# Values on shared PSUM banks, an earlier start for scores and transposes, and no filler matmuls, in a windowed attention with two MLPs

## The chip, the cores and the metric

The kernel runs on one core of a Trainium2 chip. The metric is device time in microseconds (us), the median of a few runs; lower is better. The kernel before takes 647.86 us (median of three runs, 647.62 to 649.16). The profile is one more execution, of 647.93 us.

## The reference

The input is `q`, `k`, `v` of shape (2, 8, 768, 64): 2 batches, 8 heads, 768 tokens, 64 values a head, in float32. Attention keeps, for each token, the last 128 tokens (`window`) and the first 4 tokens (`n_sink`):

```python
scores = scale * np.matmul(q, k.transpose(0, 1, 3, 2))
keep = is_sink | in_window
scores = np.where(keep, scores, -1000000000.0)
a = np.exp(scores - np.max(scores, axis=-1, keepdims=True))
a = a / (np.sum(a, axis=-1, keepdims=True) + 1e-09)
x = np.matmul(a, v)          # then (1536, 512): all tokens by heads * 64
h = x @ w_in                 # 512 -> 2048
g = np.where(h >= 1, h, np.where(h <= -1, 0.0, (h + 1) ** 2 / 4))
x = g @ w_out                # 2048 -> 512
g2 = np.maximum(x @ w2_in, 0.0) ** 2
out = g2 @ w2_out
```

`q` and `k` are scaled so that scores are large and the softmax is sharp. The weights come as float64.

## The kernel before

**Units.** The attention is cut into 24 units `(b, j, c)`: batch `b`, 256 tokens `j` of 3, and a pair of heads `c` of 4. A unit goes through this chain, on all engines:

- `turn` (L646): TensorE transposes the unit's keys and queries into a PSUM tile `tp`; `turn_copy` (L662) copies them to `k` in SBUF on VectorE (for the first unit half of it on ScalarE).
- `scores` (L671): for each half `u` of the tokens and each head `e` one matmul of `k` into a PSUM bank.
- `least` (L685, VectorE) takes scores against a mask into `p`; `powers` (L697, ScalarE) takes exponentials; `norm` (L704, VectorE) and `weigh` (L709, GpSimd) divide by the sums.
- `turn_p` (L724): TensorE transposes the probabilities into a bank `tx`; `turn_p_copy` (L735, ScalarE) copies them to `pt`, a pool of 4 buffers. Units with `j > 0` also transpose the four sink columns (`turn_s`, L740).
- `values_of` (L753): the products of values and probabilities, into `av`; `rows_high` (L773, ScalarE) and `rows_low` (L776, VectorE) split the result into two parts, `x`, in the format that the MLPs multiply.

**The MLPs.** Each product is made of three matmuls of high and low parts. The hidden layer is L371, the output L445. Four blocks of 256 tokens and two of 512 of the first MLP are mixed into the attention; all later steps are of 512 tokens.

**The order.** Everything on the fast path is written out by a planner (`Planner.run`, L171): each task has an engine, a duration (`COST`), and a priority (`KEYS` by the step of the unit, `ADJUST` by the task's number); at each step it takes the task that can start first. So each engine has one fixed order, and an instruction that waits holds back all behind it on its engine. `SLOTS` says how many buffers of each kind there are; a task that takes one is placed when one is free.

**Before the branch.** The kernel first reads `window` and `n_sink` and computes a flag; all engines load it (L1296) and branch to the fast path (L1298) or to a dense one. Ahead of the branch stand the masks, `warm_pe` matmuls of the identity (`WARM`), and the first unit's `turn` and `turn_copy`.

**PSUM.** The core has 8 banks. On the fast path two (`psf`) serve the MLPs and the second scores of the first eight units, two (`sc`) the other scores, one (`tp`) the transposes of keys and queries, two (`tx`) the transposes of probabilities, and one (`av`) the values, whose two halves are taken in turn by `c % 2`. After the attention all eight go to the MLPs.

**Filler matmuls.** Where the planner expects TensorE to be idle ahead of the first MLP task, `warm_gaps` (L1080) puts matmuls of the identity (`warm_in`, L889) into the order, so many that they should fill the gap. They write the unused last 128 columns of the latest scores' bank.

Of the kernel before, what the change touches and what calls it, by code (L numbers as in the profile page):

```python
# [8 lines left out]
F32 = mybir.dt.float32  # L9
# [6 lines left out]
PSUM = bass.MemoryType.PSUM  # L16

P = 128
# [13 lines left out]
WARM = 2, 4, 0  # L32
# [7 lines left out]
PSF, SCB, TPB, TXB = 2, 2, 1, 2  # L40
SPARE = 8
HALF = 256
SLOTS = dict(
    q=2, v=VB, k=KB, p=PB, pt=PTB, sm=4, sp=2, st=2, vs=1, av=2, sc=SCB, tp=TPB, tx=TXB, f=PSF,
# [4 lines left out]
    q=-314.28, v=162.85, kd=-162.17, kp=-309.38, tp=385.01, tpc=274.06, kp0=136.26, s0=0.28,  # L49
    m0=-70.13, e0=432.00, s1=0.64, m1=-191.77, e1=84.03, n=246.73, pm0=968.58, sp0=52.16,  # L50
    pm1=-172.01, sp1=-270.90, x0=-19.43, xc0=-212.43, x1=131.81, xc1=314.82, ts=-83.58,
    tsc=-150.73, av=453.64, xh=50.99, xl=-384.16, vs=-330.44, vc=-0.51, k1=-379.64, k2=-168.85,
)
STEPS = [
    (0, 0, -62.81, 256), (0, 256, 307.34, 256), (0, 512, 147.48, 256), (0, 768, 419.78, 256),
    (1, 0, -294.09, 512), (1, 512, 423.75, 512),
]
SPREAD = 57.03, 346.62
LOADS = [132.01, -205.46, 680.35, 143.62, -478.23, -80.53]
PARTS = [-20.40, 0.98, 33.92, 370.05, -721.81, 284.53]  # L60
START = dict(SP=4080.0, PE=6900.0, ACT=6550.0, DVE=6650.0, POOL=6850.0)
LEAD = 390.62, 134.87
# [7 lines left out]
    yl=("POOL", 690, 740, 0), yl5=("POOL", 1240, 1290, 0),  # L70
    tp=("PE", 436, 620, 0), s=("PE", 640, 709, 0), ss=("PE", 415, 492, 0), x=("PE", 436, 620, 0),
# [186 lines left out]
class Weights:  # L258
# [59 lines left out]
    def part(self, key, h, tmp):  # L318
        for _, f in self.parts(key, h, tmp):
            f()  # L320

# [261 lines left out]
class Attention:  # L583


    def __init__(self, nc, loads, ident, pools):
        self.nc, self.loads, self.ident, self.po = nc, loads, ident, pools
        self.kt, self.st, self.vs, self.spare = {}, {}, {}, None

    def go_on(self, pools, ffn):  # L590
        nc, self.po, self.ffn = self.nc, pools, ffn
        self.av = pools["av"].tile([P, 512], F32, name="av")
        self.sink_p, self.sink_t = [], []
        for i in range(2):
            t = pools["one"].tile([P, 2, 3, 32], F32, name=f"sink_p{i}")
            nc.gpsimd.memset(t, 0.0)
            self.sink_p.append(t)
            self.sink_t.append(pools["one"].tile([96, 2 * P], F32R, name=f"sink_t{i}"))
# [47 lines left out]
    def turn(self, b, j, c):  # L646
        nc, po = self.nc, self.po
        banks = 2 if po["tag"] == "f" else 1
# [22 lines left out]
    def scores(self, b, j, c, u, banks=None):  # L671
# [5 lines left out]
        for e in range(2):  # L677
            nm = f"s_{st['nm']}_{u}_{e}"
            t = self.ffn.bank(nm, banks[e]) if banks else po["sc"].tile([P, 512], F32, tag="s", name=nm)
            self.spare, ps = t[:, 3 * P :], t[:, :wid]  # L680
# [104 lines left out]
    def plan(self, line):  # L785
# [3 lines left out]
        for n, unit in enumerate(UNITS):  # L789
# [30 lines left out]
            if n:  # L820
                h = hold("tp")
                t = add("tp", key("tp"), at(self.turn), [d["q"]], [h], [raw[g]] if g in raw else [])
# [10 lines left out]
            for i in range(2):  # L833
                small = "s" if j + i == 0 else ""
                banks = [hold("f"), hold("f")] if i == 1 and n < SPARE else None
                hs = banks or [hold("sc"), hold("sc")]
                first = add(
                    "s" + small, key(f"s{i}"), at(self.scores, i, banks),
# [12 lines left out]
            sp, stt, av = hold("sp"), hold("st"), hold("av")  # L851
# [228 lines left out]
def warm_gaps(order, nc, at):  # L1080
    out, last, begun = [], START["PE"], False
    for t in order:
        if t.engine == "PE":
            begun = begun or t.kind == "mm"
            count = int((t.start - last - 250) / 225)
            if count > 0 and not begun:
                out.append((lambda c=count: warm_in(nc, at, c), False))
            last = t.start + t.step
        out.append((t.emit, any(h.pool in LATE and h.slot >= SLOTS[h.pool] for h in t.takes)))
    return out  # L1090


def fast_path(tc, nc, io, half, at, psf, masks):
    with ExitStack() as ctx:
# [22 lines left out]
        apools = dict(tag="m", vs=right("avs", 1), pt=right("apt", PTB))  # L1117
        apools.update(one=right("aone", 1), k=right("ak", KB), p=right("ap", PB), sm=right("asm", 4))
        for nm, bufs in (("sc", SCB), ("tp", TPB), ("tx", TXB), ("av", 1)):
            apools[nm] = actx.enter_context(tc.tile_pool(name=nm, bufs=bufs, space=PSUM))  # L1120
        apools["tp"] = [apools["tp"]]
# [3 lines left out]
        def open_late():  # L1125
# [4 lines left out]
            pools["psum"] += one("psf1", LATE["f"], space=PSUM)  # L1130

        with tc.manual_schedule():
            opened = False
            order = fast_plan(at, ffn, weights, stage, wtmp)
            for emit, late in warm_gaps(order, nc, at):
# [3 lines left out]
                emit()  # L1139
# [127 lines left out]
def attention_ffn_kernel(ctx, tc, q, k, v, n_sink, window, w1i, w1o, w2i, w2o, out):  # L1267
# [4 lines left out]
    psf = [ctx.enter_context(tc.tile_pool(name=f"psf{i}", bufs=1, space=PSUM)) for i in range(PSF)]  # L1272
# [8 lines left out]
    at = Attention(nc, loads, ident, dict(k=one, tp=psf, tag="f"))  # L1281
    at.keys(*UNITS[0])
    with tc.manual_schedule(engines={mybir.EngineType.DVE, mybir.EngineType.PE}):
# [11 lines left out]
        warm_pe(nc, ident, psf, "d", WARM[2])  # L1295
# [38 lines left out]
```

## Time and profile before

| what | value |
|---|---|
| median of three runs | 647.86 us (647.62 to 649.16) |
| profiled execution | 647.93 us, span of its instructions 645.5 us |
| TensorE, busy by its records | 633.8 us (98%), 3266 matmul records |
| VectorE / ScalarE / GpSimd busy | 427.1 / 324.4 / 312.2 us |
| last matmul of the attention ends, long run of MLP matmuls begins | 172.61 us |
| the first MLP matmul begins | 37.74 us |

Between the span and the execution's own time lie 2.4 us, which no instruction fills. A float32 matmul counts as two records (two passes), a matmul in the MLPs' format as one. A record of a matmul is longer than the step from its start to the next one's, since matmuls overlap; so durations on TensorE are read here from start to start. Idle time stands in brackets behind a row, with the instruction that ended it.

### The profile page before, as it was taken

How to read it: one execution, taken by the hardware profiler on the slowest of the kernel's cores; microseconds unless marked ns; L12 is line 12 of the kernel's file. 1: busy time of each engine (PE TensorE's matmuls, PEld its weight loads, DVE VectorE, ACT ScalarE, POOL GpSimd, SP SyncE). 2: the span in 40 equal slices, each digit the busy share in tenths (PEclk: the TensorE clock that was granted, in tenths of full speed). 3: DMA queues.
4: the chain of work that ended last, by engine and by line, in shares of the span. 5: the costliest groups of instructions: out<-in, count | busy, mean ns of one | idle time of the engine just before them, and what ended most of it. 6: DMA issues, size and time to landing. Idle time of an engine off the chain costs nothing.

```text
span 645.5 us, 9230 instructions
## 1 busy us (share of the span) xinstructions
PE 633.8 (98%) x3266; PEld 513.7 (80%) x3266; DVE 427.1 (66%) x855; ACT 324.4 (50%) x695; POOL 312.2 (48%) x334
## 2 busy tenths in 40 slices
PE   8999999999999999999999999999999999999996
PEld 6676887777788888888888888888888888888885
DVE  6888999753578967487889877667676564222222
ACT  4799777952555443334445564554455345212320
POOL 5569557653364444153447985544455345212311
PEclk9999999999999999999999999999999999999999
DMA  5966533200022222023221123232222220001012
GB/s 135 251 172 159 131 75 112 67 18 2 11 81 73 69 94 65 1 65 98 66 85 53 60 66 96 67 98 81 84 68 95 65 86 13 1 1 49 17 65 73
DMA packets 63901, 47.91 MB, mean 74 GB/s; under 512 B 39652, under 2 KB 58340, under 8 KB 63844
## 3 DMA queue, kind: packets, MB, share of 16 engines
q1 hardware_dynamic: 62466, 46.56, 24.9%
q10 hardware_dynamic: 1378, 0.66, 0.3%
q8 instruction: 28, 0.46, 0.3%
q14 instruction: 29, 0.24, 0.1%
HBM read 43.01 MB, written 3.15 MB: 71 GB/s over the span
## 4 chain that ended last, share of the span: by engine, by line
PE 51%; DVE 1%; ACT 0%; issue 0%; POOL 0%
PE o L445 26%; PE h L371 25%; DVE u L384 0%; POOL g L402 0%; DVE u L409 0%; ACT u L378 0%; DVE wx L313 0%; ACT wx L293 0%; DVE wx L303 0%; ACT g L398 0%; DVE wx L310 0%; DVE acc L484 0%; DVE wx L311 0%
## 5 line engine op out<-in xcount | busy, mean ns | idle before, releaser
L371 PE MATMUL h<-x,w 128*128 128x512 f32 (+1 forms) x1224 | 272.8, 378 | 0.3 <-DVE u L409 0.3
L371 PEld LDWEIGHTS h<-x,w 128*128 128x128 f32 x1224 | 220.2, 188 | 44.9 <-issue 1.0
L402 POOL TENSOR_TENSOR g<-u,g 128x512 fp32r<-128x512 f32 (+1 forms) x102 | 137.5, 1351 | 161.7 <-ACT g L398 111.5
L315 POOL TENSOR_TENSOR w<-wx,w 128x512 fp32r<-128x512 f32 x64 | 84.0, 1312 | 129.3 <-ACT w L314 115.1
L445 PE MATMUL o<-g,w 128*128 128x512 f32 (+1 forms) x648 | 140.0, 368 | 0.1
L445 PE MATMUL o<-w,g 128*128 128x512 f32 (+1 forms) x588 | 132.7, 385 | 0.0
L445 PEld LDWEIGHTS o<-g,w 128*128 128x128 f32 x648 | 112.6, 188 | 22.4 <-POOL g L402 1.1
L445 PEld LDWEIGHTS o<-w,g 128*128 128x128 f32 x588 | 108.9, 188 | 22.1
L484 DVE TENSOR_TENSOR acc<-o,acc 128x512 f32<-128x512 f32 (+1 forms) x101 | 58.1, 596 | 59.8 <-PE o L445 59.7
L314 ACT CAST w<-wx 128x512 fp32r<-128x512 f32 x64 | 39.8, 621 | 90.5 <-DVE wx L313 90.4
L398 ACT CAST g<-u 128x512 fp32r<-128x512 f32 (+1 forms) x102 | 60.3, 595 | 38.8 <-DVE u L384 21.8
L384 DVE SCALAR_TENSOR_TENSOR u<-h,u 128x512 f32<-128x512 f32 x48 | 33.0, 688 | 52.4 <-ACT u L380 52.1
L310 DVE TENSOR_SCALAR wx<-wx 128x512 f32<-128x512 f32 x64 | 39.6, 619 | 41.9 <-ACT wx L293 41.3
L313 DVE CUSTOM_DVE_ANT_0 wx<-wx,wy 128x1024 uint16<-128x1024 uint16 x64 | 60.5, 945 | 4.3
L293 ACT ACTIVATE wx<-wraw 128x512 f32<-128x512 f32 x64 | 42.8, 669 | 34.5 <-POOL w L315 33.9
L384 DVE SCALAR_TENSOR_TENSOR u<-u 128x512 f32<-128x512 f32 (+1 forms) x54 | 42.9, 795 | 25.1 <-ACT u L378 24.8
L380 ACT ACTIVATE u<-h 128x512 f32<-128x512 f32 x48 | 28.6, 596 | 61.3 <-PE h L371 61.3
L714 POOL TENSOR_TENSOR p<-p,sm 128x520 f32<-128x520 f32 (+1 forms) x48 | 48.9, 1032 | 19.4 <-DVE sm L707 16.0
L378 ACT ACTIVATE u<-h,half 128x512 f32<-128x512 f32 (+1 forms) x54 | 34.5, 638 | 47.3 <-PE h L371 46.5
L303 DVE SCALAR_TENSOR_TENSOR wx<-wraw,wx 128x512 int32<-128x512 int32 x64 | 52.4, 819 | 1.3
L700 ACT ACTIVATE p<-p,sm 128x260 f32<-128x260 f32 (+1 forms) x96 | 46.9, 490 | 8.1 <-DVE sm L692 8.1
L297 ACT ACTIVATE wy<-wraw 128x512 int32<-128x512 uint32 x64 | 42.6, 665 | 0.0
(75 smaller groups left out, 487.6 us busy)
## 6 DMA issues: line engine op xcount, KB each, us to landing
wraw<-in_moe_w_in_dram SPq DMA_DIRECT2D x32, 512.0 KB, 3.7
wraw<-in_moe_w_out_dram SPq DMA_DIRECT2D x32, 512.0 KB, 3.7
vr<-in_v_dram SPq DMA_DIRECT2D x24, 128.0 KB, 2.5
qr<-in_q_dram SPq DMA_DIRECT2D x22, 128.0 KB, 3.4
kr<-in_k_dram SPq DMA_DIRECT2D x22, 128.0 KB, 2.9
out_dram<-acc SPq DMA_DIRECT2D x10, 256.0 KB, 2.0
k<-k SPq DMA_DIRECT2D x16, 64.0 KB, 1.9
qr<-in_q_dram SPq DMA_DIRECT2D x4, 64.0 KB, 2.9
```

The costliest lines, as they stand in the source:

```text
L293: nc.scalar.activation(s["x"], f32(s["r"][:, :, 1]), AF.Abs, scale=65536.0)
L303: nc.vector.scalar_tensor_tensor(s["xi"], s["r"][:, :, 1], -(1 << 31), s["xi"], ALU.bitwise_and, ALU.bitwise_or)
L313: ("c4", lambda: nc.vector.tensor_tensor(s["xi"], s["xi"], s["yi"], ALU.add)),
L315: ("cl", lambda: nc.gpsimd.tensor_tensor(s["w"][:, 1], s["x"], f32(s["w"][:, 0]), ALU.subtract)),
L371: nc.tensor.matmul(s["h"], w[:, a, c * P : (c + 1) * P], x[:, b, c, sl], start=n == 0, stop=n == 11)
L384: nc.vector.scalar_tensor_tensor(s["u"], a, 1.0 - ffn, s["u"], op, ALU.mult)
L398: nc.scalar.copy(halves()[0], s["u"])
L402: nc.gpsimd.tensor_tensor(g[1], s["u"], f32(g[0]), ALU.subtract)
L445: nc.tensor.matmul(s["o"], lhs, rhs, start=n + i + j == 0, stop=n == len(chunks) - 1 and i == 1)
L484: self.nc.vector.tensor_tensor(dst, o, dst, ALU.add)
L700: self.nc.scalar.activation(s, s, AF.Exp, bias=sm[:, 0, u, e : e + 1], scale=-1.0, accum_out=sm[:, 1, u, e : e + 1])
L714: self.nc.gpsimd.tensor_tensor(s, s, r, ALU.mult)
```

## The change

The values lose their own bank: `values_of` takes a tile of the `tx` pool, which grows from two banks to three (`TXB`), and gives it back when `rows_low` has read it. Three banks (two of `psf` and one, `turns`, for transposes of keys and queries) become fixed tiles that exist ahead of the branch, so that the first unit's first scores and the second unit's transposes can be issued there; in the plan they are empty tasks (`go`, `gp`). `WARM` puts two more identity matmuls ahead of those scores. The filler matmuls are gone. The planner's numbers (`KEYS`, `STEPS`, `LOADS`, `ADJUST` and others) are new, so the order of all engines is new; durations in `COST` and the sizes of the steps are the same.

```diff
-WARM = 2, 4, 0
+WARM = 2, 4, 2
-PSF, SCB, TPB, TXB = 2, 2, 1, 2
+PSF, SCB, TPB, TXB = 2, 2, 1, 3
-    q=2, v=VB, k=KB, p=PB, pt=PTB, sm=4, sp=2, st=2, vs=1, av=2, sc=SCB, tp=TPB, tx=TXB, f=PSF,
+    q=2, v=VB, k=KB, p=PB, pt=PTB, sm=4, sp=2, st=2, vs=1, sc=SCB, tp=TPB, tx=TXB, f=PSF,
-    q=-314.28, v=162.85, kd=-162.17, kp=-309.38, tp=385.01, tpc=274.06, kp0=136.26, s0=0.28,
+    q=-344.78, v=165.75, kd=-209.20, kp=-262.23, tp=336.12, tpc=272.18, kp0=138.55, s0=4.70,
...
+    go=("DVE", 0, 500, 0), gp=("PE", 0, 100, 0),
...
+class Bank:
+    def __init__(self, pool, name):
+        self.all = pool.tile([P, 512], F32, name=name)
+
+    def tile(self, shape, dtype, tag, name):
+        return self.all if len(shape) == 2 else self.all.rearrange("p (n w) -> p n w", w=shape[2])
...
-        self.av = pools["av"].tile([P, 512], F32, name="av")
...
-            t = self.ffn.bank(nm, banks[e]) if banks else po["sc"].tile([P, 512], F32, tag="s", name=nm)
-            self.spare, ps = t[:, 3 * P :], t[:, :wid]
+            if banks:
+                ps = self.ffn.bank(nm, banks[e])[:, :wid]
+            else:
+                ps = po["sc"][e].tile([P, 512], F32, tag=po["tag"], name=nm)[:, :wid]
...
-        av = st["av"] = self.av[:, c % 2 * 256 : c % 2 * 256 + 256]
+        av = self.po["tx"].tile([P, 512], F32, tag="m", name=f"av_{st['nm']}")[:, :256]
+        st["av"] = av
...
-            sp, stt, av = hold("sp"), hold("st"), hold("av")
+            sp, stt, av = hold("sp"), hold("st"), hold("tx")
...
-def warm_in(nc, at, count):
-    for i in range(count if at.spare is not None else 0):
-        nc.tensor.matmul(at.spare, at.ident, at.ident, start=True, stop=True)
...
-            for emit, late in warm_gaps(order, nc, at):
+            for t in order:
+                late = any(h.pool in LATE and h.slot >= SLOTS[h.pool] for h in t.takes)
...
-        warm_pe(nc, ident, psf, "d", WARM[2])
+        warm_pe(nc, ident, [tpb], "d", WARM[2])
+        at.scores(*UNITS[0], 0)
+        at.po.update(tp=[tpb])
+        at.turn(*UNITS[1])
     fast = nc.values_load(par.flag[0:1, 0:1], min_val=0, max_val=1)
```

Three places of the new order are shown as the built programs have them. In the names the batch's number is left out: `tp_0_1_0` is the transposes' tile of `j=0, c=1`, `s_0_1_0_0` the scores of `j=0, c=1`, half 0, head 0, `kr`, `qr` and `vr` are loaded keys, queries and values, `bank` and `turns` the fixed banks; `x2` is two equal rows.

TensorE around the branch, before:

```order
L655 MATMUL tp_0_0_1_128<-ident,qr_0_0_75 128x128 x2
L1296 TENSOR_LOAD par_flag
L1297 COMPARE_AND_BRANCH
L683 MATMUL s_0_0_0_0_280<-k_0_0_89 128x128
L683 MATMUL s_0_0_0_1_282<-k_0_0_89 128x128
L655 MATMUL tp_0_1_0_284<-ident,kr_0_1_84 128x128 x2
L655 MATMUL tp_0_1_0_284<-ident,qr_0_1_81 128x128 x2
L683 MATMUL s_0_0_1_0_299<-k_0_0_89 128x260
```

TensorE around the branch, of the change:

```order
L664 MATMUL bank_65<-ident,qr_0_0_74 128x128 x2
L903 MATMUL turns<-ident 128x128 x2
L694 MATMUL bank_64<-k_0_0_89 128x128
L694 MATMUL bank_65<-k_0_0_89 128x128
L664 MATMUL turns<-ident,kr_0_1_83 128x128 x2
L664 MATMUL turns<-ident,qr_0_1_80 128x128 x2
L1301 TENSOR_LOAD par_flag
L1302 COMPARE_AND_BRANCH
L694 MATMUL bank_64<-k_0_0_89 128x260
```

Two scores and four transposes have moved ahead of the load of the flag, behind two more identity matmuls.

TensorE at the first unit's values, before (the values `av` of the first unit come behind six filler matmuls):

```order
L683 MATMUL s_1_0_1_0_482<-k_1_0_327 128x260
L683 MATMUL s_1_0_1_1_484<-k_1_0_327 128x260
L731 MATMUL tx_0_3_0_490<-ident,p_0_3_0_370 128x128
L731 MATMUL tx_0_3_0_490<-ident,p_0_3_1_418 128x128 x2
L891 MATMUL s_1_0_1_1_484<-ident 128x128 x6
L768 MATMUL av<-pt_0_0_0_398,vr_0_0_439 64x256
```

TensorE at the first unit's values, of the change:

```order
L664 MATMUL turns<-ident,qr_1_0_268 128x128 x2
L742 MATMUL tx_0_1_0_402<-ident,p_0_1_0_303 128x128
L742 MATMUL tx_0_1_0_402<-ident,p_0_1_1_321 128x128 x2
L742 MATMUL tx_0_1_1_410<-ident,p_0_1_0_303 128x128
L742 MATMUL tx_0_1_1_410<-ident,p_0_1_1_321 128x128 x2
L780 MATMUL av_0_0_417<-pt_0_0_0_370,vr_0_0_328 64x256
```

The first values now follow the transposes of the second unit, before the fourth unit's transposes and before either score of `j=1, c=0`.

SyncE's loads behind the copies of the first two units' keys, before (`vr_0_0` are the first unit's values, `wraw` the first weights):

```order
L634 DMA k_1_1_340<-k_0_1_297 128x128
L573 DMA vr_0_2_345<-in_v_dram 128x4x64 x2
L634 DMA k_1_3_361<-k_0_3_348 128x128
L272 DMA wraw_0_0_372<-in_moe_w_in_dram 128x4x256
L573 DMA qr_1_2_387<-in_q_dram 128x4x64 x2
L573 DMA kr_1_2_390<-in_k_dram 128x4x64 x2
L634 DMA k_1_2_429<-k_0_2_381 128x128
L573 DMA vr_0_0_439<-in_v_dram 128x4x64 x2
```

The same place of the change:

```order
L643 DMA k_1_1_316<-k_0_1_284 128x128
L272 DMA wraw_0_0_323<-in_moe_w_in_dram 128x4x256
L583 DMA vr_0_0_328<-in_v_dram 128x4x64 x2
L643 DMA k_1_2_341<-k_0_2_331 128x128
L583 DMA vr_0_2_352<-in_v_dram 128x4x64 x2
L583 DMA qr_1_2_375<-in_q_dram 128x4x64 x2
L583 DMA kr_1_2_378<-in_k_dram 128x4x64 x2
```

The first unit's values have moved from the last of these loads to the third, and the first weights stand ahead of them.

## Rows read from the trace of the kernel before

**Rows 1.** Busy time by stretch: us (records) of each engine, clock, DMA share, GB/s.

```profile
0.00:10.85 10.85, 8.53 (x36) 6.69 (x36) 5.45 (x27) 3.16 (x9) 4.47 (x18) 1.00 0.65 147
10.85:37.74 26.89, 24.41 (x183) 16.73 (x181) 22.93 (x86) 20.99 (x71) 17.21 (x30) 1.00 0.82 207
37.74:172.61 134.87, 132.95 (x980) 103.30 (x978) 100.19 (x299) 95.84 (x276) 84.02 (x135) 1.00 0.31 81
172.61:310.64 138.03, 137.95 (x609) 113.76 (x607) 104.26 (x158) 63.47 (x104) 58.41 (x42) 1.00 0.21 65
```

**Rows 2.** The chain that ended last, its last two pieces: start, us, what.

```profile
629.58 11.04 PE o L445 x60
640.65 0.42 DVE acc L484
```

**Rows 3.** Timeline of TensorE around the branch: start, us, line, shapes, count.

```profile
6.91 0.80 PE L683 MATMUL s<-k 64*128 64x128 f32 x4 [0.61 <-DVE k L669]
7.64 0.69 PE L655 MATMUL tp<-ident,kr 128*128 128x128 f32 x2
...
8.68 1.67 PE L683 MATMUL s<-k 64*128 64x260 f32 x8
...
11.60 0.44 PE L655 MATMUL tp<-ident,kr 128*128 128x128 f32 x2
```

**Rows 4.** Timeline of GpSimd and VectorE around the branch.

```profile
5.45 0.29 POOL L923 COPY mask<-mask 128x128 f32<-128x128 f32 x1
6.10 0.45 POOL L596 MEMSET sink_p<- 128x192 f32 x2 [0.36 <-issue]
...
6.34 0.42 DVE L669 COPY k<-tp 128x256 f32<-128x256 f32 x1 [1.26 <-PE tp L655]
7.14 0.69 DVE L927 TENSOR_SCALAR mask<-mask 128x260 f32<-128x260 f32 x2 [0.37 <-POOL vsr L606]
...
9.96 0.43 DVE L692 CUSTOM_DVE_ANT_0 p<-s,mask 128x260 f32<-128x260 f32 x1 [0.47 <-PE s L683]
```

**Rows 5.** Timeline of TensorE at three stretches of filler matmuls (L891).

```profile
12.67 0.94 PE L891 MATMUL s<-ident 128*128 128x128 f32 x6 [0.41 <-DVE sm L692]
13.53 0.49 PE L683 MATMUL s<-k 64*128 64x128 f32 x4
...
20.97 0.55 PE L731 MATMUL tx<-ident,p 128*128 128x128 f32 x3
22.08 1.60 PE L891 MATMUL s<-ident 128*128 128x128 f32 x12 [0.56 <-DVE sm L692]
23.61 0.87 PE L768 MATMUL av<-pt,vr 128*64 128x256 f32 x8
...
27.06 0.87 PE L768 MATMUL av<-pt,vr 128*64 128x256 f32 x8
27.86 0.49 PE L891 MATMUL s<-ident 128*128 128x128 f32 x2
28.55 0.55 PE L731 MATMUL tx<-ident,p 128*128 128x128 f32 x3 [0.20 <-ACT pt L738]
28.94 0.38 PE L655 MATMUL tp<-ident,kr 128*128 128x128 f32 x2
```

**Rows 6.** Timeline of SyncE's queue: the issues of the first unit's values.

```profile
17.76 1.26 SPq L573 DMA_DIRECT2D vr<-in_v_dram  x2
```

**Rows 7.** The page's part on DMA issues: KB each, median us to landing.

```profile
vr<-in_v_dram SPq DMA_DIRECT2D x24, 128.0 KB, 2.5
```

**Rows 8.** Timeline of ScalarE and VectorE behind those stretches.

```profile
24.90 0.48 ACT L738 COPY pt<-tx 128x384 f32<-128x384 f32 x1 [1.37 <-PE av L768]
...
29.57 0.69 DVE L669 COPY k<-tp 128x512 f32<-128x512 f32 x1 [1.47 <-PE tp L655]
...
30.97 0.42 DVE L778 TENSOR_TENSOR x<-av,x 128x256 fp32r<-128x256 f32 x1
```

**Rows 9.** TensorE's waits from 37.74 to 172.61: us in total, times, longest.

```profile
PE ts L744 <- ACT pt L738: 0.3, 1, 0.3
```

More of the change, by code (lines that the diff above doesn't have):

```diff
@@ L48 @@
 KEYS = dict(
-    q=-314.28, v=162.85, kd=-162.17, kp=-309.38, tp=385.01, tpc=274.06, kp0=136.26, s0=0.28,
-    m0=-70.13, e0=432.00, s1=0.64, m1=-191.77, e1=84.03, n=246.73, pm0=968.58, sp0=52.16,
-    pm1=-172.01, sp1=-270.90, x0=-19.43, xc0=-212.43, x1=131.81, xc1=314.82, ts=-83.58,
-    tsc=-150.73, av=453.64, xh=50.99, xl=-384.16, vs=-330.44, vc=-0.51, k1=-379.64, k2=-168.85,
+    q=-344.78, v=165.75, kd=-209.20, kp=-262.23, tp=336.12, tpc=272.18, kp0=138.55, s0=4.70,
+    m0=-55.92, e0=490.71, s1=5.10, m1=-212.00, e1=112.49, n=200.32, pm0=935.74, sp0=37.11,
+    pm1=-189.91, sp1=-267.39, x0=-37.13, xc0=-221.23, x1=47.20, xc1=294.51, ts=3.54, tsc=-141.44,
+    av=437.63, xh=94.26, xl=-436.35, vs=-351.47, vc=28.84, k1=-354.91, k2=-81.86,
 )
 STEPS = [
-    (0, 0, -62.81, 256), (0, 256, 307.34, 256), (0, 512, 147.48, 256), (0, 768, 419.78, 256),
-    (1, 0, -294.09, 512), (1, 512, 423.75, 512),
-]
[L58 to L62, printed above, removed]
+    (0, 0, -52.86, 256), (0, 256, 267.55, 256), (0, 512, 185.85, 256), (0, 768, 401.71, 256),
+    (1, 0, -317.67, 512), (1, 512, 447.76, 512),
+]
+SPREAD = 52.75, 365.29
+LOADS = [114.00, -193.13, 635.31, 131.49, -461.22, -127.44]
+PARTS = [-17.08, 65.94, -2.94, 420.96, -785.29, 338.10]
+START = dict(SP=4080.0, PE=8100.0, ACT=6450.0, DVE=6950.0, POOL=6050.0)
+LEAD = 388.63, 141.49
 LAG = dict(PE=53, ACT=33, DVE=33, POOL=78, SP=40)
@@ L587, in __init__ @@
         self.nc, self.loads, self.ident, self.po = nc, loads, ident, pools
-        self.kt, self.st, self.vs, self.spare = {}, {}, {}, None
+        self.kt, self.st, self.vs = {}, {}, {}
     def go_on(self, pools, ffn):
         nc, self.po, self.ffn = self.nc, pools, ffn
-        self.av = pools["av"].tile([P, 512], F32, name="av")
         self.sink_p, self.sink_t = [], []
@@ L647, in turn @@
         nc, po = self.nc, self.po
-        banks = 2 if po["tag"] == "f" else 1
+        banks = len(po["tp"])
         ps = [
@@ L820, in plan @@
             if n:
-                h = hold("tp")
-                t = add("tp", key("tp"), at(self.turn), [d["q"]], [h], [raw[g]] if g in raw else [])
+                h, begun = hold("tp"), n == 1
+                t = add(
+                    "gp" if begun else "tp", key("tp"), (lambda: None) if begun else at(self.turn),
+                    [d["q"]], [h], [raw[g]] if g in raw else [],
+                )
                 d["tpc"] = add(
@@ L834, in plan @@
                 small = "s" if j + i == 0 else ""
-                banks = [hold("f"), hold("f")] if i == 1 and n < SPARE else None
+                begun = n + i == 0
+                banks = [hold("f"), hold("f")] if begun or i == 1 and n < SPARE else None
                 hs = banks or [hold("sc"), hold("sc")]
                 first = add(
-                    "s" + small, key(f"s{i}"), at(self.scores, i, banks),
+                    "go" if begun else "s" + small, key(f"s{i}"),
+                    (lambda: None) if begun else at(self.scores, i, banks),
                     [d["tpc"], d["kp"] if j + i else None, d.get("kd")], hs, [kt],
@@ L1077, in fast_plan @@
     return line.run()
[L1080 to L1090, printed above, removed]
 def fast_path(tc, nc, io, half, at, psf, masks):
@@ L1116, in fast_path @@
         at.loads.pool = right("araw", 2)
-        apools = dict(tag="m", vs=right("avs", 1), pt=right("apt", PTB))
+        apools = dict(tag="f", vs=right("avs", 1), pt=right("apt", PTB))
         apools.update(one=right("aone", 1), k=right("ak", KB), p=right("ap", PB), sm=right("asm", 4))
-        for nm, bufs in (("sc", SCB), ("tp", TPB), ("tx", TXB), ("av", 1)):
+        for nm, bufs in (("sc", SCB), ("tx", TXB)):
             apools[nm] = actx.enter_context(tc.tile_pool(name=nm, bufs=bufs, space=PSUM))
-        apools["tp"] = [apools["tp"]]
+        apools["sc"], apools["tp"] = [apools["sc"]] * 2, at.po["tp"]
         at.go_on(apools, ffn)
@@ L1129, in open_late @@
             pools["tmps"]["U"] = left("tmp1", LATE["U"], side="right")
-            pools["psum"] += one("psf1", LATE["f"], space=PSUM)
+            pools["psum"] += at.po["tp"] + one("psf1", LATE["f"] - TPB, space=PSUM)
         with tc.manual_schedule():
@@ L1138, in fast_path @@
                     opened = True
-                emit()
+                t.emit()
 def dense_masks(nc, pool, par):
@@ L1271, in attention_ffn_kernel @@
     first = ctx.enter_context(tc.tile_pool(name="first", bufs=2))
-    psf = [ctx.enter_context(tc.tile_pool(name=f"psf{i}", bufs=1, space=PSUM)) for i in range(PSF)]
+    banks = ctx.enter_context(tc.tile_pool(name="banks", bufs=1, space=PSUM))
+    psf = [Bank(banks, f"bank{i}") for i in range(PSF)]
     loads = Loads(nc, first, io)
@@ L1280, in attention_ffn_kernel @@
     warm = one.tile([P, 1], F32, name="warm")
-    at = Attention(nc, loads, ident, dict(k=one, tp=psf, tag="f"))
+    tpb = Bank(banks, "turns")
+    at = Attention(nc, loads, ident, dict(k=one, tp=psf, sc=psf, tag="f"))
     at.keys(*UNITS[0])
```

27 rows, old and new, of tables (ADJUST, SWITCH) are left out of this document.

## The prediction

> **What bounds the kernel now.** I read the profile in this order: busy time by stretch, the chain that ended last, then the timeline of the first 38 us engine by engine, and TensorE's waits behind that.
>
> The busy times by stretch show where time can be won at all [rows 1]. From 172.61 us, the end of the attention, to 310.64 us TensorE is busy 137.95 of 138.03 us: it waits for nothing, and this goes on to the end, where 60 matmuls of the output layer are followed only by VectorE's last sum at 640.65 us [rows 2]. So the last 468.0 us (640.65 - 172.61) are a solid block of TensorE work. In both orders the same MLP work stands ahead of the attention's last matmul (counted in them: 288 matmuls of 256 columns and 100 of 512), so this block is the same after the change, and whatever the change does must move the 172.61 us at its front. The execution's own time, 647.93 us, is this end plus what lies around the span; it is 0.07 us above the median of the runs shown, which is nothing here.
>
> In front of the block TensorE waits 134.87 - 132.95 = 1.9 us between 37.74 and 172.61 us, and 26.89 - 24.41 = 2.5 us between 10.85 and 37.74 us [rows 1]. To the latter come the filler matmuls, which count as busy and do no work. Of the other engines VectorE is the fullest in that stretch: 22.93 of 26.89 us, 4.0 us idle. The stretch can't shrink by more than these 4.0 us unless VectorE gets less to do.
>
> Before 11 us TensorE runs at the lower of its two rates: two transposes take 0.69 us at 7.64 us and 0.44 us at 11.60 us [rows 3].
>
> **The change part by part.**
>
> *The branch (A).* Before, TensorE branches in the 0.61 us in which it waits for the first keys' copy anyway [rows 3], so it costs nothing. Now it branches behind the second unit's transposes. The scores themselves can't start sooner: they wait for VectorE's copy, which ends at 6.34 + 0.42 = 6.76 us [rows 4], and nothing ahead of that copy changes. So the first scores and the transposes keep their times, and the branch stands exposed between the transposes and the second scores, which begin at 8.68 us. A branch costs GpSimd 0.36 us (between its rows at 5.45 and 6.10) and VectorE 0.37 us [rows 4]; on TensorE it lies between nothing and the whole 0.61 us. Behind it VectorE's next step waits 0.47 us for just these scores [rows 4], so a delay is passed on. The two identity matmuls are four passes; the four of the transposes take 8.68 - 7.64 = 1.04 us, so these reach at most 0.43 us beyond the wait of 0.61. On the other side, if denser work raised the rate sooner, four passes would win 0.1 us each and the eight of the scores at 8.68, which take 1.67 us, up to 0.8 us. Bounds -1.2 to +1.0 us; I take +0.2, half of the branch, since its load can begin while the transposes ahead still run.
>
> *The filler matmuls (B).* Three of their five stretches are shown [rows 5]. From 12.67 to 13.53 us they take 0.86 us, after a wait of 0.41 us of their own: they write the bank that VectorE still reads. The scores behind them start without any wait, so they were ready before. From 22.08 to 23.61 us they take 1.53 us after a wait of 0.56. The transposes ahead end at 20.97 + 0.55 = 21.52 us, and the first values start at 23.61, again without a wait of their own. What do these need? Their loads were issued from 17.76 us for 1.26 us [rows 6], and take 2.5 us to land [rows 7]: 21.5 us. So the values could have begun 2.1 us sooner. It mattered: ScalarE's next copy waits 1.37 us for exactly these matmuls [rows 8], since they free one of the four `pt` buffers. The third stretch, 27.86 to 28.55 us, ends in a wait for ScalarE (0.20 us), so there the filler itself cost little, but ScalarE was late for the same reason, and VectorE behind it waits 1.47 us [rows 8]. The change takes the fillers out, loads those values two places earlier in SyncE's queue and puts their product ahead of the fourth unit's transposes. I take 0.3 of the first 0.86 us, 1.7 of the second stretch's 2.1, and 0.4 of the third's 0.69: -2.4 us. Bounds: nothing, if another engine is late instead, and -4.0 us, all that VectorE can give.
>
> *Three banks for transposes and values (C).* The bank of the transposes was late twice in the rows: 0.20 us at 28.55 [rows 5] and 0.3 us later on [rows 9]; with a third bank some 0.3 us of this goes. Against it, the values hold a bank until VectorE has read them: those that start at 27.06 us are read until 30.97 + 0.42 = 31.39 us, 4.3 us [rows 5, 8]. Four takers a unit now share three banks; before, three shared two, and the values had two halves. Some transposes will now wait for VectorE's `rows_low`, and behind them the scores and values queued on TensorE. Between nothing and 0.2 us (the wait above) for each of 24 units, 4.8 us; since waits of this kind were as rare as that before, I take +0.4. C is +0.1 us.
>
> *The new order (D, E).* A transpose that follows scores costs more: 0.44 us for two against 0.38 us where another transpose is ahead [rows 3, 5]. Scores are followed by transposes 25 times in the order before and 16 times in the new one: 9 x 0.06 = -0.5 us (D; bounds 0 and -0.9). For the 1.9 us of waits behind 37.74 us no row says which way a new order moves them: 0, with 1.9 us on both sides (E).
>
> *The sum:* +0.2 - 2.4 + 0.1 - 0.5 = -2.6 us; 647.93 - 2.6 = **645.3 us**. What is late next is VectorE, whose 4.0 us of idle time would be down to about 1.5.
>
> **The rivals.**
>
> *VectorE hides it* (no change). It is 85% busy from 10.85 to 37.74 us and ScalarE 78% [rows 1]; some of its idle time is a wait that any order has. Then B gives only half of the 1.47 us that VectorE waits at 29.57, 0.7 instead of 2.4 us: 645.3 + 1.7 = 647.0 us. For it speaks how full both are; against it that the wait of 1.37 us on ScalarE and the 1.47 us on VectorE both lead back to the late values.
>
> *Values block the banks* (slower). TensorE stands at a transpose whose bank VectorE has not yet freed, 0.2 us in each of 24 units, in place of the 0.4 in C: 645.3 + 4.4 = 649.7 us, and more if each wait is longer. It decides from 0.1 us a unit on, where 2.4 us eat B. For it: 4.3 us of holding, and an in-order engine. Against it: before, with as many takers for each bank, TensorE hardly ever waited for one.
>
> *TensorE's rate.* The fillers kept TensorE at work in its pauses. Without them the lower rate may last longer, or return. The work from 11.60 to 12.67 us, 1.1 us [rows 3, 5], would take twice as long, and half as much once more in a later pause: 645.3 + 1.6 = 646.9 us. Against it: the granted clock reads 1.00, the level of 2.4 GHz, from 10.85 us on in spite of waits of half a microsecond [rows 1]. (It reads 1.00 ahead of that too, where transposes take twice as long, the level of 1.2 GHz; so the early rate is read from spacings.) The Trainium skill, in TensorE: Matmul & The Clock Gate, section on PE-mode transpose, says that transposes do not count as activity in the way that matmuls do; by that rule the change, which leaves transposes and scores alone there, would stay slow longer, and 646.9 us is what it makes. No run here separates the two yet: the rate rose behind a mix of transposes, scores and a filler.
>
> *More is won.* Denser work ahead of the branch raises the rate sooner (A at -1.2 instead of +0.2): 645.3 - 1.4 = 643.9 us.
>
> **How the numbers follow.** Forecast 0.43, with its own range 644.3 to 646.5 us (B between -1.4 and -3.3, the rest about as taken); VectorE hides it 0.25; values block 0.13; rate 0.07; more is won 0.12. What a measurement of this kernel can tell from no change is about 0.3%, 1.9 us: below 645.9 is faster, above 649.8 slower. Faster: three quarters of the forecast's 0.43, all of the 0.12, a fifth of 0.25, 0.01 of the rate: 0.32 + 0.12 + 0.05 + 0.01 = 0.50. Slower: half of 0.13, since 649.7 lies on the border, and 0.05 for E on its bad side with C: 0.12. No difference: the rest, 0.38. The range: below 642.6 us only A, B and E together at their good ends would lead; above 649.4 us lies a good half of the blocked banks. 642.6 to 649.4 us.
>
> **What would show it.** A: TensorE's second scores begin at about 8.9 us behind the branch, not earlier than 8.7; earlier means that the rate rose sooner, with transposes of 0.44 us for two ahead of the branch. B: the first values' product begins before 20 us, ScalarE's copies behind it do not wait a microsecond for TensorE, and the first MLP matmul begins some 2 us before 37.74 us. C: waits of transposes (`tx`) or values for `rows_low` in TensorE's list of waits, in sum under half a microsecond; 2 us or more there is the slower rival. The attention's last matmul ends at about 170 us, and from there to the last sum it is 468 us as now; if that part changes, the frame of this prediction is wrong. It is also wrong if the attention's end moves and the first MLP matmul does not, or the other way round: then E decided.

## The result, and the profile after

| | before | after |
|---|---|---|
| median of runs on one chip, us | 648.26 (647.62 to 649.16, 4 runs) | 642.39 (642.04 to 643.83, 4 runs) |
| ratio to before | 1 | 0.9913 [0.9893, 0.9933] |
| profiled execution and its span, us | 647.93, 645.5 | 642.04, 640.2 |
| first MLP matmul starts, us | 37.74 | 33.15 |
| attention's last matmul ends, us | 172.61 | 167.20 |
| from there to the last sum, us | 468.04 | 468.04 |

The kernel is 0.87% faster; the forecast was 645.3 us, 0.40%, in a range from 642.6 to 649.4 and with a chance of 0.50 for faster. The sign was right, and the gain came out about twice as large: 642.39 us lies 0.2 us below the range. The gain lies where it was looked for. The busy times by stretch answer to [rows 1] (us, then busy time and records of TensorE, its weight loads, VectorE, ScalarE and GpSimd, clock, DMA share, GB/s):

```profile
10.85:33.15 22.30, 19.73 (x158) 13.47 (x156) 21.65 (x83) 20.45 (x71) 16.94 (x31) 1.00 0.98 245
33.15:167.20 134.05, 132.67 (x976) 103.36 (x973) 98.89 (x298) 95.52 (x271) 84.43 (x133) 1.00 0.32 82
167.20:305.23 138.03, 137.82 (x608) 113.72 (x607) 107.20 (x163) 66.95 (x110) 58.92 (x42) 1.00 0.25 77
```

The front stretch is 4.6 us shorter, the middle one 0.8, the rest is as it was: the chain that ended last now closes with

```profile
633.77 1.45 PE o L455 x12
635.22 0.02 issue
635.24 0.42 DVE acc L494
```

and 635.24 - 167.20 is the same 468.04 us as 640.65 - 172.61 [rows 1, 2]. In the front stretch VectorE, with 4.0 us idle before, is now busy 21.65 of 22.30 us: 0.65 us is left to win there without taking work from it. The stretch shrank by 4.6 us, more than the 4.0 that the prediction held possible, since it also has 1.3 us less of VectorE's work in it (22.93 before; 83 instructions instead of 86).

TensorE's timeline around the branch and at the first values, to be laid beside [rows 3, 5]:

```profile
6.11 1.05 PE L903 MATMUL turns<-ident 128*128 128x128 f32 x4
7.08 0.49 PE L694 MATMUL bank<-k 64*128 64x128 f32 x4
7.51 0.44 PE L664 MATMUL turns<-ident,kr 128*128 128x128 f32 x2
7.78 0.38 PE L664 MATMUL turns<-ident,qr 128*128 128x128 f32 x2
8.19 0.82 PE L694 MATMUL bank<-k 64*128 64x260 f32 x4
...
10.38 0.44 PE L664 MATMUL turns<-ident,kr 128*128 128x128 f32 x2
...
12.22 0.49 PE L694 MATMUL s<-k 64*128 64x128 f32 x4 [1.19 <-DVE k L678]
...
16.32 0.87 PE L780 MATMUL av<-pt,vr 128*64 128x256 f32 x8
...
22.36 0.71 PE L694 MATMUL s<-k 64*128 64x260 f32 x4 [1.19 <-DVE k L678]
```

Two transposes take 0.44 us already at 7.51 us, where they took 0.69 at 7.64 [rows 3]: TensorE runs at the higher rate from about 7.0 us here, and from about 10.9 in the execution before. The second scores begin at 8.19 instead of 8.68 us, the first values at 16.32 instead of 23.61. TensorE's list of waits, whole program (us in total, times, longest):

```profile
PE s L694 <- DVE k L678: 2.4, 2, 1.2
PE bank L903 <- POOL ident masks.py:199: 1.7, 1, 1.7
PE s L694 <- DVE sm L703: 1.1, 1, 1.1
PE o L455 <- POOL g L412: 0.2, 1, 0.2
```

No transpose and no value product stands in it with a wait for a bank, and the wait of [rows 9] is gone. In SyncE's queue the first unit's values are issued at 11.85 us, behind the first weights, where it was 17.76 [rows 6]; the pair at 13.51 is the third unit's, which before stood ahead of them:

```profile
11.85 1.05 SPq L583 DMA_DIRECT2D vr<-in_v_dram  x2
12.99 0.47 SPq L643 DMA_DIRECT2D k<-k  x1
13.51 1.14 SPq L583 DMA_DIRECT2D vr<-in_v_dram  x2
```

### The profile page after: what moved, and what is told of

Read it like the earlier page. It is cut to its first block, busy times and chain, and to the rows that moved or that the text cites. A ratio compares the mean times of both kernels' runs of the same rounds, so it can differ in the third digit from the quotient of the medians.

```text
span 640.2 us, 9164 instructions
## 1 busy us (share of the span) xinstructions
PE 629.3 (98%) x3246; PEld 511.3 (80%) x3246; DVE 424.8 (66%) x855; ACT 324.0 (51%) x695; POOL 313.4 (49%) x334
## 4 chain that ended last, share of the span: by engine, by line
PE 90%; DVE 4%; ACT 3%; POOL 1%; issue 1%; DMA 1%; SPq 0%; DVEq 0%; POOLq 0%; ACTq 0%
PE h L381 26%; PE o L455 21%; PE bank L381 13%; PE bank L455 13%; PE turns L455 8%; PE av L780 3%; PE s L694 2%; PE tx L742 2%; ACT p L711 1%; DVE p L703 1%; PE turns L381 1%; PE turns L664 1%; DMA wraw<-in_moe_w_in_dram 1%; ACT pt L749 1%; PE bank L903 1%
## 5 line engine op out<-in xcount | busy, mean ns | idle before, releaser
L381 PE MATMUL h<-x,w 128*128 128x512 f32 x768 | 181.3, 389 | 0.0
L381 PEld LDWEIGHTS h<-x,w 128*128 128x128 f32 x768 | 144.2, 188 | 30.0
L381 PE MATMUL bank<-x,w 128*128 128x512 f32 (+1 forms) x432 | 90.5, 358 | 0.0
L381 PEld LDWEIGHTS bank<-x,w 128*128 128x128 f32 x432 | 71.4, 189 | 12.8 <-issue 1.4
L455 PE MATMUL o<-w,g 128*128 128x512 f32 (+1 forms) x300 | 73.9, 385 | 0.0
L455 PE MATMUL o<-g,w 128*128 128x512 f32 x297 | 73.0, 390 | 0.2 <-POOL g L412 0.2
L455 PEld LDWEIGHTS o<-g,w 128*128 128x128 f32 x297 | 55.6, 188 | 12.3 <-POOL g L412 0.6
L455 PEld LDWEIGHTS o<-w,g 128*128 128x128 f32 x300 | 55.6, 188 | 11.3
L494 DVE TENSOR_TENSOR acc<-o,acc 128x512 f32<-128x512 f32 (+1 forms) x56 | 32.1, 586 | 37.6 <-PE o L455 37.4
L455 PE MATMUL bank<-g,w 128*128 128x256 f32 (+1 forms) x276 | 54.5, 339 | 0.0
```

What stands on the lines that cost most here:

```text
L381: nc.tensor.matmul(s["h"], w[:, a, c * P : (c + 1) * P], x[:, b, c, sl], start=n == 0, stop=n == 11)
L455: nc.tensor.matmul(s["o"], lhs, rhs, start=n + i + j == 0, stop=n == len(chunks) - 1 and i == 1)
```

## The experiments

The theory after the result: fillers out, shared banks and the new order each win about a microsecond or two, and the early start adds an earlier rate of TensorE. The rival: the rate wins it all, or the order alone. Times of one kernel turned out to fall in groups, above all those of before (646.2, 647.5 and 648.8 us), so the groups are told with the medians. The granted clock of each run, over its whole span, helps to tell them apart: in the two profiled runs in which the lower rate came back (last section) it is 0.996 and 0.997, in all other profiled runs 0.998 to 1.000. A run with 0.997 or less is counted below as one in which the lower rate came back, by that sign and not by a profile of its own. Ratios are to before, timed beside each kernel.

**Fillers out, all else as before.**

```
-            if count > 0 and not begun:
+            if count > 0 and not begun and False:
```

> The kernel before, its order and its banks, without its 12 filler matmuls. Working theory: of the 5.4 us that the attention's end moved (172.6 to 167.2 us), the fillers alone hold some 2 us, since the first values wait behind them from 21.5 to 23.6 us; the order holds the rest: 646.2 us here, with the first values at about 21.7 us and the first MLP matmul at about 36. Rival 'the fillers are all of it apart from the early rate': 644 us. Rival 'the fillers filled air' (VectorE sets the pace, as in the prediction's case without a change): 648 us, the first MLP matmul at 37.7. Rival 'the fillers kept the rate': above 648.5 us and transposes of 0.69 us for two behind 11 us.

Measured: 646.24 us (644.61 to 648.42, 12 runs), ratio 0.9976 [0.9960, 0.9992]. Groups near 644.9, 646.2 and 648.4; the runs at 646.18 and 646.31 have a granted clock of 0.997. That the median meets the expected 646.2 is in part luck, since it lies in the middle one of three groups. The profiled run is of the last: its first scores behind the branch, and its transposes until 15 us, go at the lower rate.

```profile
11.96 0.69 PE L655 MATMUL tp<-ident,kr 128*128 128x128 f32 x2
...
15.07 0.63 PE L655 MATMUL tp<-ident,qr 128*128 128x128 f32 x2
...
18.51 0.47 PE L655 MATMUL tp<-ident,kr 128*128 128x128 f32 x2
```

So the fillers cost some 1.3 us by the medians (647.49 for before beside it) and by the earliest groups. That they bring the rate up sooner is not shown. In the profiled run of before it rose behind a first filler at 10.28 us, and here, without it, at 18.5; but the latest group (648.3 us and above) holds 4 of 12 runs here and 8 of 23 of before.

**The first scores and second transposes behind the branch, no identity matmuls; and the identity matmuls alone taken out.** Both from the kernel after.

```
-WARM = 2, 4, 2
+WARM = 2, 4, 0
-        at.scores(*UNITS[0], 0)
-        at.turn(*UNITS[1])
```

(the last two lines, with the planner's tasks that issue these two instead, in the first kernel only)

> The changed kernel, with the first unit's first scores and the second unit's transposes behind the branch again, and without the two identity matmuls ahead of it; order and banks else as changed. Working theory: the denser work ahead of the branch raised TensorE's rate at 7.0 instead of 10.8 us of the span, worth about 1.2 us (the second unit's third step stands at 10.38 instead of 11.60): 643.6 us here, two transposes 0.69 us at 7.6 us. Rival 'the early start is worth nothing by the end, since VectorE is full behind it': 642.4 us. Rival 'the early start is most of the gain': 646 us or more.

> The changed kernel without the two identity matmuls ahead of the first scores; the rest stays ahead of the branch. Working theory: those four passes close the one pause in TensorE's work from 1.7 us on, and with the pause the rate rises only at about 10.8 us: 643.6 us, as with all of it behind the branch. Rival 'the moved scores and transposes do it': 642.4 us, the rate up at 7 us. Rival 'the phase of the rate's rise is chance and has nothing to do with this': the rise at 7 or at 10.8 us whatever stands there, and 642.4 to 643.6 us.

Measured: 643.51 (643.30 to 645.34, 6 runs), 0.9935 [0.9916, 0.9953]; and 643.86 (642.08 to 645.68, 6 runs), 0.9930 [0.9906, 0.9954]. Both profiled runs (645.04 and 645.46 us) are at the lower rate until 18.5 to 18.9 us, and in both the first MLP matmul starts at 36.33 us: at the same rate the early start moves nothing. Both medians come near the expected 643.6 by luck: neither profile shows a rise at 10.8 us. Four runs of the first kernel lie at 643.3 to 643.6 with a granted clock of 0.997, two at 645.0 to 645.3; three runs of the kernel without identity matmuls lie at 642.1 to 642.6, where the kernel after lies, three at 645.1 to 645.7. These matmuls therefore change how often the rate is early, not what an early one gives. Over all experiments and the kernel after, 69 of 72 runs with identity matmuls lie ahead of the latest group of their kernel; of the 36 without them and without fillers 20 do.

**The new order with the values in a bank of their own**, in two halves, and two banks for the transposes, as before. With this edit the output differs from the reference's (relative error 0.05), and which instruction makes the difference is not shown; its time alone is used.

```
-        av = self.po["tx"].tile([P, 512], F32, tag="m", ...)[:, :256]
+        av = st["av"] = self.av[:, c % 2 * 256 : c % 2 * 256 + 256]
-        for nm, bufs in (("sc", SCB), ("tx", TXB)):
+        for nm, bufs in (("sc", SCB), ("tx", 2), ("av", 1)):
```

> The changed kernel, same order on every engine, but the values have a bank of their own again, whose halves are taken in turn, and transposes of probabilities two banks. Working theory: the third bank frees TensorE of waits on ScalarE's copies, some 0.3 us, and its values block little: 642.7 us. Rival 'the shared banks make the order possible': several waits of TensorE for ScalarE's copies (tx) of half a microsecond and more, 645 us or above. Rival 'values block the banks': 641.9 us or less, without them.

Measured: 647.52 (647.27 to 648.47, 12 runs), ratio 1.0002 [0.9990, 1.0014]: the whole gain is gone, as in the rival 'the shared banks make the order possible' and not as in the theory, although the rate is early in its profiled run (two transposes in 0.56 us at 7.82, 0.44 from 10.74). TensorE's waits from 34 us on show where:

```profile
PE tx L743 <- ACT pt L750: 2.1, 4, 0.8
PE bank L455 <- DVE acc L492: 1.0, 1, 1.0
PE s L695 <- DVE sm L704: 0.9, 1, 0.9
PE ts L756 <- ACT pt L750: 0.8, 2, 0.4
PE bank L381 <- DVE u L419: 0.3, 1, 0.3
```

2.1 + 0.8 us are transposes that wait until ScalarE has emptied one of two banks. Its middle stretch takes 138.73 us against 134.05 in the kernel after; these waits are 2.9 of the 4.7 us, and 1.0 + 0.3 more are waits for VectorE that the list of the kernel after doesn't have:

```profile
34.13:172.86 138.73, 133.39 (x977) 103.16 (x975) 99.04 (x296) 96.39 (x270) 83.28 (x133) 1.00 0.30 80
```

**The shared banks in the order of before**, without fillers.

```
-        av = st["av"] = self.av[:, c % 2 * 256 : c % 2 * 256 + 256]
+        av = self.po["tx"].tile([P, 512], F32, tag="m", ...)[:, :256]
+        st["av"] = av
-        for nm, bufs in (("sc", SCB), ("tp", TPB), ("tx", TXB), ("av", 1)):
+        for nm, bufs in (("sc", SCB), ("tp", TPB), ("tx", TXB + 1)):
```

> The order of before without its fillers, with the values' product drawn from one pool of three banks that it shares with the transposes of probabilities (before: two banks for these, one for the values in two halves). Theory (the shared banks are worth time only with the new order, which needs a third bank for the transposes): within 0.5 us of the run without fillers, so 646 us and a ratio of 0.997 to 0.998. Rival (the third bank by itself frees the transposes, whatever the order): 1 to 3 us below the run without fillers, 643.5 to 645 us. Slower rival (values hold banks that the old order's transposes come back to): above 648 us, with waits of transposes for VectorE's rows_low.

Measured: 646.63 (643.45 to 647.22, 12 runs), ratio 0.9975 [0.9957, 0.9992]. By the median the theory holds; by the groups it does not: three runs near 643.5, two near 645.0 (granted clock 0.995 and 0.996) and seven from 646.5 to 647.2, each group 1.2 to 1.4 us below one of the kernel without fillers, with more of the runs in the late one. The two profiled runs (647.22 and 648.42 us, both at the lower rate until 18.5 us) say the same. TensorE's waits from 38 us on without shared banks:

```profile
PE av L768 <- ACT sink_t L751: 0.6, 2, 0.5
PE tx L731 <- POOL p L714: 0.4, 2, 0.2
PE ts L744 <- ACT pt L738: 0.3, 1, 0.3
PE h L371 <- DVE u L409: 0.3, 1, 0.3
```

And with them, where the wait of `ts` for a bank is gone:

```profile
PE av L768 <- ACT sink_t L750: 0.9, 3, 0.5
PE tx L730 <- POOL p L713: 0.4, 2, 0.2
PE h L371 <- DVE u L409: 0.3, 1, 0.3
```

That wait is 0.3 us, and the waits for `sink_t` grow by as much. The stretch from the first MLP matmul to the attention's end is shorter by 0.76 us all the same (134.89 and 134.13 us), and the one ahead of it by 0.54 (the first MLP matmul at 38.56 and 38.02): that the shared banks win is shown, through which waits is mostly not. The median had hidden a gain behind the rate. Hence the rest of the runs, in which the rate is made early.

**Identity matmuls alone, in the kernel before; six instead of two in the kernel after; and the kernel after once more.**

```
-WARM = 2, 4, 0
+WARM = 2, 4, 2
```

(the first; `WARM = 2, 4, 6` in the second)

> The kernel before with two identity matmuls ahead of the branch, and nothing else changed. Theory (they only raise the odds that TensorE's rate rises early; before's times fall near 646.2, 647.5 and 648.7 us by the moment of that rise): the lowest times stay near 646.2, more of them lie there, median 646.2 to 647.0, ratio 0.998 to 1.000. Rival (they are plain work on the path): every group 0.3 to 0.5 us later, ratio above 1.000. Rival (no effect on the rate): the same spread as before, ratio 1.000.

> The changed kernel with six identity matmuls ahead of the first scores where it has two. Theory (the early rise is already had in most runs with two, and four more delay the first scores by up to 0.4 us at the lower rate): 642.0 to 642.8 us, ratio about 0.992, nearly all times in one group. Rival (the rise still fails in part of the runs, and denser work mends that): median below that of the changed kernel run beside it by 0.5 us or more. Rival (no bearing on the rate): two groups, near 642 and 645 us, as without identity matmuls.

> The changed kernel once more, beside the other three on one chip, to see its times in more runs. Theory (two identity matmuls make the early rise likely, not certain): most times near 642.0 to 642.5 and a few at 643.8 or above; median 642.3, ratio 0.992. Rival (the rise is a matter of the run and not of these matmuls): half of the times near 645, as without them, median above 643.

Measured: 646.45 (646.28 to 649.21, 12 runs), ratio 0.9996 [0.9983, 1.0008]; 644.55 (643.90 to 645.00, 8 runs), 0.9955 [0.9940, 0.9971]; 642.12 (641.97 to 643.24, 6 runs), 0.9924 [0.9906, 0.9942]. In the kernel before, two identity matmuls put 11 of 12 runs between 646.28 and 646.93 us, where 15 of 25 of the kernel itself lay, and leave the lowest time where it was. Of six, the four more delay the scores: these start at 8.52 us instead of 6.94, and the time is 2.4 us longer (1.9 by the lowest times). The delay is not all of it: five of the eight runs have a granted clock of 0.996, so the lower rate came back in them. The expected 642.0 to 642.8 was a miss, since in it I had priced them at 0.4 us.

```profile
6.10 2.49 PE L903 MATMUL turns<-ident 128*128 128x128 f32 x12
8.52 0.49 PE L694 MATMUL bank<-k 64*128 64x128 f32 x4
```

**The parts one by one, all with the two identity matmuls.** Before without fillers; with the shared banks as well; and the new order as well, with the first scores and second transposes still behind the branch (the edits as above).

> The kernel before without its fillers and with two identity matmuls ahead of the branch. Theory (the identity matmuls put nearly every run into the group with the early rate, the parts of the change then add up in that group): one group near 644.6 to 645.0 us, the lowest group of the run without fillers. Rival (the fillers carry the rate, without them the identity matmuls don't hold it): times spread up to 648.4 as without fillers, median above 645.8.

> As the run with identity matmuls and no fillers, and the values share three banks with the transposes; still the order of before. Theory (the parts add): one group near 643.5 us, 1.1 us below the run with two and one banks. Rival (the shared banks gave the low times of the earlier run by chance of the rate): the same time as with two and one banks, within 0.3 us.

> The changed kernel with its identity matmuls, but with the first scores and the second unit's transposes behind the branch, as before. Theory (the early start itself is worth nothing, and what it seemed to be worth was the rate): one group at 642.0 to 642.4 us. Rival (the early start is worth 1 us or more by itself): one group at 643.3 us, the lowest group without both.

| with two identity matmuls | median, us (lowest to highest, runs) | ratio to before | step, us |
|---|---|---|---|
| kernel before | 646.45 (646.28 to 649.21, 12) | 0.9996 [0.9983, 1.0008] | |
| fillers out | 645.27 (644.81 to 648.61, 12) | 0.9974 [0.9959, 0.9989] | -1.2 |
| shared banks | 644.32 (643.50 to 647.33, 12) | 0.9961 [0.9948, 0.9975] | -0.95 |
| new order | 642.45 (642.07 to 643.14, 6) | 0.9926 [0.9910, 0.9942] | -1.9 |
| early start: the kernel after | 642.12 (641.97 to 643.24, 6) | 0.9924 [0.9906, 0.9942] | -0.3 |

The first and last row ran on another chip than the three between (before: 646.44 and 646.64 us beside them), so the outer steps are good to some 0.2 us by that, and the intervals of neighbours overlap. But the four profiled runs at the lower rate until 18.5 to 18.9 us give like steps: 648.42 without fillers, 647.22 with shared banks (-1.2), 645.04 with the new order (-2.2), 645.46 with the early start (+0.4). So do the runs with an early rate that stayed (without those at 0.997 or less and the one late run of each of the first three kernels): medians of 646.44, 645.10, 644.04, 642.28 and 642.08 us, steps of -1.3, -1.1, -1.8 and -0.2. The early start is worth nothing that can be told from 0. The steps hold for this sequence only: the new order without the third bank takes 647.52 us, 2.2 more than the old order without it (645.27), and there the bank is worth 5.4.

The expectation of one group failed twice. The times without fillers form two, 644.8 to 645.4 and 646.4 to 646.5, with one at 648.61; those with shared banks as well lie at 643.5 to 644.4 and, with a granted clock of 0.996 or 0.997, at 644.8 to 645.2, with one at 647.33. The profiled run without fillers (646.52) shows a second cause. With the early rate the values come due before their load has landed, since in the order of before it stands late in SyncE's queue, and behind that wait TensorE is at the lower rate (granted clock 0.50 from 21.35 to 24.77 us):

```profile
21.33 1.55 PE L768 MATMUL av<-pt,vr 128*64 128x256 f32 x8 [1.13 <-DMA vr<-in_v_dram]
22.81 2.09 PE L683 MATMUL s<-k 64*128 64x260 f32 x8
```

SyncE's row of that load, issued 4.1 us ahead:

```profile
17.22 1.16 SPq L573 DMA_DIRECT2D vr<-in_v_dram  x2
```

The new order issues these loads at 11.85 us and has no such wait.

## Why the prediction was right in its direction, and where its sizes were off

*The frame* held to the hundredth: the block behind the attention is 468.04 us in both, TensorE's gain is all ahead of it, and VectorE is next in the way (0.65 us idle in the front stretch, forecast about 1.5).

*A, the branch and the early start (+0.2, bounds -1.2 to +1.0).* The exposed branch cannot be seen: -0.3 us in one comparison, +0.4 in the other. With the early rate, TensorE's second scores begin at 8.19 us with the branch just ahead of them (first row, the kernel after in its second profile) and with the early start taken out (second row): in both they wait until VectorE has read the first scores out of their bank.

```profile
8.19 0.82 PE L694 MATMUL bank<-k 64*128 64x260 f32 x4 [0.16 <-DVE sm L703]
8.19 0.82 PE L694 MATMUL bank<-k 64*128 64x260 f32 x4 [0.24 <-DVE sm L703]
```

So neither the branch nor the start ahead of it was on the path there. The 0.37 us that I took for VectorE's branch is, by its own row [rows 4], a wait for GpSimd's `vsr`. What the identity matmuls do is make the rate's early rise the usual case. In the pair of profiled runs that shows as 647.93 - 646.29 = 1.6 us (the kernel before, in its profiled run and in that with identity matmuls). This is the part that the rival "more is won" named, with the mechanism that it named.

*B, D and E, fillers out, switches and the new order (-2.4, -0.5 and 0, together -2.9).* Measured -1.2 for the fillers and -1.9 (-2.2 at the late rate) for the order, which holds the earlier values: together -3.1 to -3.4. The values' part of the argument, late loads and late copies behind them [rows 5, 6, 8], is borne out by the wait of 1.13 us for `vr` where the loads stay late. The sizes of B were not. With two identity matmuls the first values begin at 22.56 us with the fillers and at 21.33 without, 1.2 us sooner and not 1.7 to 2.1, since the load then ends the wait. And the 0.3 us of the first stretch had no ground: there the scores were not ready before, they need VectorE's copy (with the fillers, then without, both with identity matmuls):

```profile
12.52 0.49 PE L683 MATMUL s<-k 64*128 64x128 f32 x4
12.65 0.49 PE L683 MATMUL s<-k 64*128 64x128 f32 x4 [1.19 <-DVE k L669]
```

What the switches give by themselves (D) was not tried.

*C, three banks (+0.1) is the step that failed.* I took 0.3 us for the third bank, from the two waits that the rows of before show, and paid 0.4 for the values that hold one. Measured: -0.95 to -1.2 us in the old order; and without it the new order loses 647.52 - 642.12 = 5.4 us. The waits of before were few in its own order, which was planned with two banks; in an order planned with three, the same two banks cost 5.4 us. The trace of before could not show that price. My range had no room for it either, since C's best end was the 0.3 us; with C at its measured size the time came to lie below it. That the values block little, the other half of C, held, although they hold their banks about as long as before: the first unit's from 16.32 to 18.67 + 0.42 = 19.09 us, 2.8 us against 2.5 before (from 23.61 to 26.10), the second unit's 3.9 us against the 4.3 that I had counted [rows 5, 8]. The first row is of before, the others of the kernel after:

```profile
25.68 0.42 DVE L778 TENSOR_TENSOR x<-av,x 128x256 fp32r<-128x256 f32 x1 [0.15 <-ACT x L774]
...
18.67 0.42 DVE L790 TENSOR_TENSOR x<-av,x 128x256 fp32r<-128x256 f32 x1
18.78 0.94 PE L780 MATMUL av<-pt,vr 128*64 128x256 f32 x8
...
22.22 0.41 DVE L790 TENSOR_TENSOR x<-av,x 128x256 fp32r<-128x256 f32 x1
```

*The sum* at the same, early rate: 646.45 - 642.12 = 4.3 us measured, 2.6 forecast. Of the difference of 1.7 us, by the steps of the table, 1.05 is C, 0.5 is A and 0.2 is B, D and E. The profiled pair shows 5.9, the 1.6 more being the rate.

*The rivals.* VectorE did not hide it, though it came close to being full. Values do not block the banks: no wait of that kind stands in the list. TensorE's rate, forecast with 0.07 as a loss, is real in both its halves, but not in the kernel after as a rule: without fillers and without identity matmuls the lower rate lasts to 18.5 us in part of the runs, and two of ten runs of the kernel after (643.24 and 643.83 us) lost the higher one again, by their granted clock of 0.997. The Trainium skill, in TensorE: Matmul & The Clock Gate, section on PE-mode transpose, says that transposes do not count as busy time in the way that matmuls do. The trace agrees in so far as nearly half of TensorE's work from 5.2 us to the late rise is transposes (some 5 of 11 us in the profile without fillers), and two identity matmuls, two real matmuls in place of a pause, bring the rise to 6.1 to 8.2 us in all eight profiled runs that have them. It does not prove the rule, since the pause went with them, and since 20 of 36 runs rose early without them.

## What to carry to other kernels

Before a wait that hardly occurs is taken as cheap, ask what order was chosen to avoid it: more buffers are worth what a new order makes of them, and that shows only when order and buffers are tried apart. Where times fall in groups, compare group with group, or first remove the cause of the groups (here two matmuls in an idle pause), and only then price the parts. And look at which loads a gain of two microseconds makes late.

## What the runs showed of the hardware

TensorE's higher rate (granted clock 1.00, the level of 2.4 GHz) began at 6.1 to 8.2, 10.9 or 18.5 to 18.9 us in the profiled runs of kernels that do the same work until 5.9 us: the first with identity matmuls, the other two without. The times of a single kernel fall into groups that fit such moments (646.2, 647.5 and 648.8 us for before); for before the first two are shown by profiles, with and without identity matmuls, and the third is not. I had expected one moment for each kernel.

The lower rate also came back, in two of the eleven profiled runs of the experiments. In the kernel with the new order and the scores behind the branch, two transposes take 0.38 us at 10.65 us and 0.62 us at 12.92, behind a wait of 1.19 us for VectorE, and the usual 0.44 and 0.38 again from 16.35 on; the granted clock is 0.50, the level of 1.2 GHz, from 12.92 to 16.33 us. The first row has its four passes of identity at the higher rate already (1.05 us in the kernel after):

```profile
6.10 0.61 PE L903 MATMUL turns<-ident 128*128 128x128 f32 x4
...
10.65 0.38 PE L664 MATMUL turns<-ident,qr 128*128 128x128 f32 x2
12.22 0.49 PE L694 MATMUL s<-k 64*128 64x128 f32 x4 [1.19 <-DVE k L678]
12.64 0.47 PE L664 MATMUL turns<-ident,kr 128*128 128x128 f32 x2
12.92 0.62 PE L664 MATMUL turns<-ident,qr 128*128 128x128 f32 x2
13.34 1.49 PE L742 MATMUL tx<-ident,p 128*128 128x128 f32 x6
...
16.35 0.44 PE L664 MATMUL turns<-ident,kr 128*128 128x128 f32 x2
```

The other is the run without fillers above, where eight value matmuls take 1.55 instead of 0.87 us behind the wait for their load. The kernel after has the same wait of 1.19 us at the same place and kept the rate behind it in both of its profiled runs, and so did four other profiled runs with a wait of 1.18 or 1.19 us there. So a pause of a microsecond can cost the rate, and does not have to; what decides it stays open. The granted clock reads 1.00 ahead of the first rise, too, where spacings show half the rate: its record begins only with that rise (at 7.01 us in the profile of the kernel after, at 10.85 in that of before), and what lies ahead of it counts as 1.00. So the early part is read from spacings, the later one from either.
